# A new written order for the first two chunks of a hash-masked attention and MLP kernel, with two transpose banks and casts out of PSUM

## The chip, the cores and the metric

The kernel runs on one core of one Trainium2 chip. The metric is the device time of an execution in microseconds (us); a kernel's time is the median of its runs. A profile is one execution taken by the hardware profiler. Engines are TensorE (PE, with its weight loads as PEld), VectorE (DVE), ScalarE (ACT), GpSimd (POOL) and SyncE (SP). DMAs are issued from SP, ACT or POOL.

## The reference

Four batches, eight heads, 768 positions, head dimension 64. Queries and keys are hashed by the signs of six projections; a key counts for a query only if all six bits agree. The heads are then joined to rows of 512 and go through a normalised two-layer MLP with a residual.

```python
q_bits = (np.einsum('bhsd,dk->bhsk', q, proj) > 0)          # k_bits likewise
mask = q_bucket[:, :, :, None] == k_bucket[:, :, None, :]
scores = np.where(mask, scale * np.matmul(q, k.transpose(0, 1, 3, 2)), -1e9)
attn = np.exp(scores - np.max(scores, axis=-1, keepdims=True))
attn = attn / (np.sum(attn, axis=-1, keepdims=True) + 1e-09)
x = np.matmul(attn, v)                 # heads joined: (4, 768, 512)
xn = (x - mu) / np.sqrt(var + 1e-06) * g_ln
out = x + np.maximum(xn @ w_ch1, 0.0) @ w_ch2
```

## The kernel before

The work is cut into twelve chunks (batch, third), each of 2 x 128 query positions. A chunk's attention is twelve units: `scores` (four matmuls of 256 columns into one of two `sc` tiles), `exps` on ACT, `values` (eight matmuls into `av`) and, every third unit, `divide` on DVE. The mask is part of the scores: the six bits stand as extra rows under the 64 rows of transposed queries and keys in the operand tile `slots0` or `slots1` (even and odd batches), so that a matmul over 70 rows makes score and agreement together. A chunk's MLP (`norm`, eight `up` products with a relu, eight `down` products) runs between the units of the next chunk. From chunk 2 on `interleave` spreads it there together with the preparation of the next batch, which the strings in `steps` place by letters.

Batch 0 and batch 1 are prepared in different ways.

For batch 0 everything is made on the engines, in `first_two`, and the order of the first two chunks is written out by hand in the string `opening`. Each word is one step, in the order in which the engines get their instructions; every engine then works its own queue in order. For a head h, `T` (`transposes`) makes three key blocks and one query block by four PE transposes into a PSUM tile `tpose` of tag `av1`; `E` (`scaled`) copies that to an SBUF tile `qkT` or `spare` with a factor; `C` (`cast`) copies half of it, 64 x 512, from SBUF into `slots0` as bf16; `H` (`hash_two`) multiplies two heads with the projection; `B` (`compare`) turns the products into bits; `O` (`odd_bits`) copies a 6 x 512 strip of bits. The letter behind a word names the engine: a for ACT, d for DVE, g for POOL. `LT`, `LE`, `LC`, `LH`, `LB`, `LO` do the same for the later query blocks of two heads. `S`, `X`, `V`, `D` are the four parts of a unit. `K` are matmuls on constants that keep PE awake, `J` copies the projection, `vc`, `su`, `sd` prepare the values. `n`, `xt`, `xe`, `nr`, `U`, `R` are the MLP of chunk 0 up to its relus. `V` and `T` share the tag `av1`: the first chunk's `av` is in `av0` alone, the second's alternate.

The word `w` issues loads from POOL's queue: `w0` the first MLP weight (two DMAs), `w1` the queries and keys of batch 1, first half, `w2` the second weight (two DMAs), `w3` the second half's queries and keys and the first half's values. The loads of batch 0 go from SP and two from ACT.

For batch 1 and later the operands are made by DMA. `na` (`narrow`) casts a half's queries and keys to bf16 on POOL (into `nat16`, one buffer, which the last three `qkT` of batch 0 share as `spare`). `op` is `operands`, a DMA transpose into `slots1`, and `shifted`, a DMA that moves its upper rows; both are issued from SP. `bl` (`blocks`) are DVE block transposes of the fp32 data, `hashes` multiplies them with the projection and writes the bits to DRAM (`bits_d`), and `bit_rows` reads them back in four DMAs. In the string of chunk 2 the second half follows: narrowing, transpose (`T11`), values (`W11`), shift (`P11`), hashes (`H11`), bit rows (`J11`). In the string of chunk 3, `n` issues the DMA transpose `xnT` of chunk 2's normalised rows, and the next word `L20` loads batch 2, all from SP's queue in that order:

```python
        2: "n d d H10 d d x N11 J10 d N11 B11 d T11 B11 V10 d B11 W11 d B11 u P11 u H11 u J11 E10 u V11 u u u u",
        3: "n L20 d d d d W20 d E11 d N20 d N20 B20 d T20 B20 u B20 u B20 u P20 u u u u u",
```

Of the kernel before, what the change touches and what calls it, by code (L numbers as in the profile page):

```python
# [9 lines left out]
F32 = mybir.dt.float32  # L10
# [20 lines left out]
def kernel(  # L31
# [11 lines left out]
    nc = tc.nc  # L43
# [16 lines left out]
    consts = ctx.enter_context(tc.tile_pool(name="consts", bufs=1))  # L60


    wake = consts.tile([P, P], BF16)
    nc.vector.memset(wake, 2.0 / P)
    wake2 = consts.tile([P, 2], BF16)
    nc.vector.memset(wake2, 0.0)

    proj1 = consts.tile([P, D], F32)
    nc.vector.memset(proj1, 0.0)
    identf = consts.tile([P, P], F32)  # L70
    make_identity(nc, identf)
    nc.gpsimd.dma_start(out=proj1[0:D, 0:n_bits], in_=proj)
    expb = consts.tile([P, 2], F32)
    nc.gpsimd.memset(expb[:, 0:1], -scale * n_bits * 0.25 / Q_SCALE)
    nc.gpsimd.memset(expb[:, 1:2], -scale * n_bits * LBIT)
# [51 lines left out]
    def load_half(b, half):  # L127

        h0 = half * H // 2
        t = {}  # L130
        for nm in "qk":
            t[nm] = nat.tile([P, H // 2, NC, D], F32, tag=f"{nm}nat", name=f"{nm}nat")

        cuts = [[0, 1, 2, 4] if half == 0 else [0, 2, 4], [0, 4], [0, 2, 4], [0, 2, 4]][b]
        for lo, hi in zip(cuts, cuts[1:]):
            for nm, src in (("q", q), ("k", k)):
                eng = nc.gpsimd if b == 1 else nc.scalar if nm == "k" and hi - lo == 1 else nc.sync
                eng.dma_start(
                    out=t[nm][:, lo:hi],
                    in_=src[b, h0 + lo : h0 + hi].rearrange("h (p c) d -> p h c d", p=P),  # L140
                )
        if b == 0 and half == 0:
            nc.scalar.activation(wake2[:, 0:1], wake2[:, 1:2], AF.Exp)
            t["v"] = load_values(b, half)
        return t
# [16 lines left out]
    class Prep:  # L162


        def __init__(self, b):
            self.b, self.tiles = b, {}
            self.sl, self.va, self.vs = slots[b % 2], vaug[b % 2], vsum[b % 2]
            self.qkT, self.nat16, self.bt = {}, {}, {}

        def load(self, half):  # L170
            self.tiles.setdefault(half, {}).update(load_half(self.b, half))
# [16 lines left out]

            return self.sl.rearrange("p h a (c t) -> p h (a c) t", t=P)

        def transposes(self, key):

            tp = ps_av.tile([P, 4, P], F32, tag="av1", name="tpose")
            late = isinstance(key, tuple)
            for g in range(4):
                if late:
                    h, nm, c = 2 * key[1] + g // 2, "q", 2 + 2 * (g % 2)
                else:
                    h, nm, c = key, "kkkq"[g], 2 * (g % 3)
                nc.tensor.transpose(  # L200
                    tp[:, g, :],
                    self.tiles[h // 4][nm][:, h % 4, c : c + 2].rearrange("p c d -> p (c d)"),
                    identf,
                )
            self.bt[key] = tp

        def scaled(self, key, engine):

# [30 lines left out]

        def cast(self, key, par, engine):  # L240

            self.copy_by(
                engine,
                self.places(key, slice(0, D), par),
                self.as_placed(key, self.qkT[key][par * D : (par + 1) * D]),
            )

        def hash_two(self, keys):

# [25 lines left out]

        def narrow(self, half, a):

            if a == 0:
                self.nat16[half] = work.tile(
                    [P, H // 2, 2, NC, D], BF16, tag="nat16", bufs=1, name="nat16"  # L280
                )
            nc.gpsimd.tensor_copy(self.nat16[half][:, :, a], self.tiles[half]["qk"[a]])  # L282
# [134 lines left out]
    def att_units(b, t, x):  # L417
# [15 lines left out]
        for j in range(NP):  # L433
# [7 lines left out]
            for g, grp in enumerate(groups):  # L441
# [18 lines left out]
                    )  # L460
                    state[g] = ex

                def values(grp=grp, g=g, state=state, j=j, ha=ha):
                    if g == 0:
                        slot = 0 if (b, t) == (0, 0) else j % 2
                        av = ps_av.tile([P, 2, TT, D1], F32, tag=f"av{slot}", name="av")
                        state["av"] = av
                        if b == 0:
                            nc.tensor.matmul(
                                av,  # L470
                                epsk,
                                vsplit[:, ha : ha + 2, :].unsqueeze(2).to_broadcast(
                                    [P, 2, TT, D1]
                                ),
                                start=True, stop=False, skip_group_check=True,
                            )
# [39 lines left out]
    def mlp_steps(b, t, x):  # L516
        st = {}
        steps = []

        def norm_rows(i):  # L520

            if i == 0:
                st["xn"] = work.tile([P, ND, TT, P], BF16, tag="xn", bufs=1, name="xn")
                st["mv"] = work.tile([P, TT, 2], F32, tag="mv", name="mv")
            xn, mv = st["xn"], st["mv"]
            stats = work.tile([P, 6], F32, tag="stats", bufs=4, name="stats")
            nc.vector.bn_stats(stats, x[:, i, :])  # L527
            nc.vector.bn_aggr(mv[:, i, :], stats)  # L528
            nc.vector.scalar_tensor_tensor(  # L529
                xn[:, :, i, :],  # L530
                x[:, i, :].rearrange("p (o d) -> p o d", d=P),
                mv[:, i, 0:1],
                gbc.rearrange("p (o d) -> p o d", d=P),
                op0=AOP.subtract, op1=AOP.mult,
            )
# [6 lines left out]

        def norm():

            for i in range(TT):
                norm_rows(i)
            if b or t > 1:
                xnT = work.tile([P, ND, CT], BF16, tag="xnT", bufs=1, name="xnT")
                nc.sync.dma_start_transpose(
# [12 lines left out]
                        tp[:, dt, i * P : (i + 1) * P], st["xn"][:, dt, i, :], ident  # L562
                    )

        def xcopy():

            st["xnT"] = work.tile([P, ND, CT], BF16, tag="xnT", bufs=1, name="xnT")
            nc.vector.tensor_copy(st["xnT"], st["tp"])

        def up_products(n2):  # L570
            if n2 == 0:
# [41 lines left out]
        def down(i, part):  # L613
# [20 lines left out]
            (870, lambda i=i, part=part: down(i, part)) for i in range(TT) for part in range(4)  # L634
        ]
        parts = {
            "rows": norm_rows, "scale": norm_scale, "xt": xtrans, "xe": xcopy,
            "up": up_products, "relu": rectify, "columns": down_columns,
        }

# [86 lines left out]
    def chunk_tile():  # L727
# [4 lines left out]
    mlp = {0: mlp_steps(*chunks[0], xs[0])}  # L732

    opening = """
        K26 T0 E0a C0.0a C0.1d K6 T1 E1a C1.1a C1.0d K10 J0 H0 K10 T2 B0 E2a B1 O0a K8 T3 C2.0g
        O1d S0 E3a C2.1d vc0 w0 S1 X0 C3.1d H1 C3.0d X1 su0 B2 T4 sd0 S2 O2a E4a B3 S3 V0 X2
        C4.0g O3d T5 C4.1d V1 w1 E5a V2 S4 X3 C5.0d H2 C5.1d vc1 D2 X4 LT2 B4 S5 LE2a su1 B5 O4g
        X5 T6 O5g sd1 S6 V3 LC2.1g E6a LC2.0d S7 X6 C6.1d C6.0g T7 V4 w2 E7d V5 X7 S8 C7.0d H3
        C7.1d X8 D5 LT0 B6 V6 LE0a V7 B7 O6g LT1 O7d LC0.0g S9 LE1d LC0.1g V8 S10 X9 LC1.1d LH0
        w3 D8 X10 LC1.0d S11 LB0 V9 X11 V10 LO0d LT3 LB1 S12 LE3a V11 LO1d S13 X12 LC3.0g D11  # L740
        LH1 n0 LC3.1g X13 S14 V12 X14 V13 n1 S15 X15 V14 S16 LB2 xt0 nr0 X16 D14 V15 xe0 S17
        LO2g V16 LB3 X17 U0 LO3d S18 R0d U1 na0 X18 bl3 S19 U2 R1a bl0 X19 S20 R2d U3 na1 op0
        bl1 V17 S21 R3a D17 V18 X20 U4 bl2 V19 X21 U5 R4d S22 R5a V20 S23 X22 D20 V21 U6 X23 V22
        S24 R6d V23 X24 U7 D23 R7a
    """

    def first_two():
# [6 lines left out]
        nc.sync.dma_start(out=gbc, in_=moe_g_ln.partition_broadcast(P))  # L754
        every = units[0] + units[1] + units[2][:1]
        parts = mlp[0][4]
        engines = {"a": nc.scalar, "d": nc.vector, "g": nc.gpsimd}

        def keep_awake(n):
            tp = ps_mm.tile([P, P], F32, tag="mm", name="wakep")  # L760
# [19 lines left out]
        def both(i):  # L780
# [2 lines left out]
        table = {  # L783
            "K": lambda n: keep_awake(n),
            "J": lambda n: first_head_projection(),
            "T": lambda h: prep.transposes(h),
            "E": lambda h, e: prep.scaled(h, e),
            "C": lambda h, par, e: prep.cast(h, par, e),
            "H": lambda j: prep.hash_two([2 * j, 2 * j + 1]),
            "B": lambda h: prep.compare(h),  # L790
            "O": lambda h, e: prep.odd_bits(h, e),
            "LT": lambda j: prep.transposes(("late", j)),
            "LE": lambda j, e: prep.scaled(("late", j), e),
            "LC": lambda j, par, e: prep.cast(("late", j), par, e),
            "LH": lambda i: prep.hash_two(both(i)),
# [4 lines left out]
            "V": lambda u: every[u][2](),  # L800
# [5 lines left out]
            "n": lambda i: parts["rows"](i),  # L806
            "nr": lambda _: parts["scale"](),
            "xt": lambda _: parts["xt"](),
            "xe": lambda _: parts["xe"](),
# [4 lines left out]
            "op": lambda _: (nxt.operands(0), nxt.shifted(0)),  # L814
        }
        for word in opening.split():
            name = word.rstrip("0123456789.adg") if word[-1] in "adg" else word.rstrip("0123456789.")
            rest = word[len(name) :]
            engine = [engines[rest[-1]]] if rest[-1] in engines else []
            numbers = [int(x) for x in rest.rstrip("adg").split(".")]  # L820
            table[name](*numbers, *engine)


# [275 lines left out]
```

## Time and profile before

| | us |
|---|---|
| median of 3 runs | 314.08 (313.74 to 314.28) |
| the profiled execution | 312.45 |
| its span, first to last instruction | 310.6 |
| PE busy | 299.4 (96%) |
| ACT busy | 217.2 (70%) |
| DVE busy | 184.6 (59%) |
| POOL busy | 84.7 (27%) |
| granted TensorE clock, mean | 1.00 |

The first opening score matmul starts at 10.94, the last hidden product of chunk 0 (`U7`) at 50.51, and chunk 3 begins at about 78. Busy shares are means over the whole span; in the first 45 us PE is the engine that waits, after that it hardly does. In a line of the timeline the columns are start, duration, engine (SPq is SP's queue), line, operation, output and inputs with shapes, count, and in brackets the idle time before it and what ended it. An issuing instruction's duration is that of the issue, not of the transfer.

### The profile page before, as it was taken

To read this page: it belongs to the slowest core of one execution; us is meant where nothing else is said; L and a number is where in the kernel's file an instruction comes from. 1 tells how busy PE (TensorE), PEld (TensorE's weight loads), DVE (VectorE), ACT (ScalarE), POOL (GpSimd) and SP (SyncE) were. 2 spreads that over 40 slices of the span, in tenths; PEclk is the share of its full clock that TensorE was granted. 3 is DMA by queue.
4 is the path that set the end of the run, shared out by engine and by line. 5 is a ranking of instruction groups with operands and counts; after the bars stand their busy time and mean duration, and the time that the engine had idled before them with its cause. 6 is when DMAs were issued, how large, how long until landed. Compare 5 with 4: busy or idle time off the path is not lost.

```text
span 310.6 us, 7810 instructions
## 1 busy us (share of the span) xinstructions
PE 299.4 (96%) x3241; PEld 226.0 (73%) x3268; DVE 184.6 (59%) x404; ACT 217.2 (70%) x272; POOL 84.7 (27%) x110
## 2 busy tenths in 40 slices
PE   7979999999999999999999999999999999999995
PEld 6656787678669678678679668669679678688574
DVE  1799996654665756743793694653643734734522
ACT  5677977775798777688788778778778677666020
POOL 3467530914321118151290470100100100100200
PEclk9999999999999999999999999999999999999999
DMA  7999998487396476695199637030030110200302
GB/s 237 374 208 304 211 339 129 103 124 185 52 313 156 93 245 119 130 273 154 64 262 154 171 76 168 19 76 37 1 102 0 35 71 0 69 36 0 104 0 77
DMA packets 64970, 40.93 MB, mean 132 GB/s; under 512 B 47153, under 2 KB 59953, under 8 KB 64929
## 3 DMA queue, kind: packets, MB, share of 16 engines
q1 hardware_dynamic: 60224, 31.59, 41.1%
q0 software_dynamic: 4128, 8.13, 11.1%
q10 hardware_dynamic: 576, 0.66, 0.6%
q8 instruction: 27, 0.44, 0.6%
q14 instruction: 15, 0.11, 0.1%
HBM read 27.98 MB, written 6.88 MB: 112 GB/s over the span
## 4 chain that ended last, share of the span: by engine, by line
PE 84%; DVE 9%; ACT 3%; issue 2%; DMA 1%; POOL 0%; SPq 0%; ACTq 0%; POOLq 0%
PE hp L577 26%; PE o L618 22%; PE sc L446 18%; PE av L480 10%; PE hash L321 3%; DVE slots L262 2%; PE tpose L200 1%; DVE slots L238 1%; DVE bt L287 1%; PE wakep L762 1%; PE o L600 1%; PE hash L252 1%; DMA xnT<-xn 1%; DVE xn L529 1%; DVE x L508 1%
## 5 line engine op out<-in xcount | busy, mean ns | idle before, releaser
L456 ACT ACTIVATE ex<-sc,expb 128x1024 bf16<-128x1024 f32 x144 | 159.5, 1113 | 56.5 <-PE sc L446 54.0
L577 PE MATMUL hp<-xnT,w_sb 128*128 128x256 bf16 x768 | 98.7, 272 | 1.6 <-DVE hbuf L587 0.9
L618 PE MATMUL o<-w_sb,hbuf 128*128 128x512 bf16 x341 | 89.6, 379 | 1.2
L446 PE MATMUL sc<-slots 70*128 70x256 bf16 x576 | 86.5, 272 | 2.2 <-POOL slots L238 1.5
L577 PEld LDWEIGHTS <-w_sb 128*128 128x128 bf16 x768 | 72.0, 97 | 11.2 <-issue 2.4
L480 PEld LDWEIGHTS <-ex 128*128 128x128 bf16 x1152 | 54.0, 98 | 15.7 <-ACT ex L456 1.6
L446 PEld LDWEIGHTS <-slots 70*128 70x128 bf16 x576 | 51.8, 97 | 17.2 <-issue 3.7
L480 PE MATMUL av<-vaug,ex 128*128 128x65 bf16 x1152 | 58.8, 194 | 0.3 <-ACT ex L456 0.2
L587 DVE TENSOR_SCALAR hbuf<-hp 128x512 bf16<-128x512 f32 x48 | 32.8, 684 | 43.6 <-PE hp L577 42.5
L618 PEld LDWEIGHTS <-hbuf 128*128 128x128 bf16 x368 | 33.6, 97 | 25.5
L540 POOL TENSOR_SCALAR rs<-mv 128x2 f32<-128x2 f32 x12 | 9.1, 759 | 155.2 <-DVE mv L528 155.2
L589 ACT ACTIVATE hbuf<-hp 128x512 bf16<-128x512 f32 x48 | 28.5, 594 | 20.2 <-PE hp L577 20.2
L623 DVE SCALAR_TENSOR_TENSOR x<-o,rs,x 128x512 f32<-128x512 f32 x23 | 17.1, 744 | 26.4 <-PE o L618 23.5
L529 DVE SCALAR_TENSOR_TENSOR xn<-x,mv,gbc 128x512 bf16<-128x512 f32 x24 | 17.9, 751 | 0.8
L508 DVE TENSOR_TENSOR x<-x,rc 128x256 f32<-128x256 f32 x36 | 16.8, 466 | 1.2
L500 DVE TENSOR_SCALAR rc<-av 128x4 f32<-128x4 f32 x36 | 5.7, 158 | 19.8 <-PE av L480 19.8
L527 DVE BATCH_NORM_STATS2 stats<-x 128x6 f32<-128x512 f32 x24 | 16.5, 690 | 0.4
L351 POOL CAST vaug<-vnat 128x1536 bf16<-128x1536 f32 x8 | 12.0, 1494 | 15.6 <-DMA vnat<-in_v_dram 15.6
L501 DVE TENSOR_TENSOR x<-av,vsum 128x256 f32<-128x256 f32 x36 | 14.9, 414 | 0.0
L282 POOL CAST nat<-qnat 128x1536 bf16<-128x1536 f32 x6 | 8.8, 1470 | 16.8 <-issue 8.8
L180 ACT ACTIVATE knat<-knat 128x768 f32<-128x768 f32 x16 | 13.4, 836 | 0.0
L180 ACT ACTIVATE qnat<-qnat 128x768 f32<-128x768 f32 x16 | 13.3, 833 | 0.0
(86 smaller groups left out, 215.9 us busy)
## 6 DMA issues: line engine op xcount, KB each, us to landing
out_dram<-x SPq DMA_DIRECT2D x23, 256.0 KB
vnat<-in_v_dram SPq DMA_DIRECT2D x7, 768.0 KB
qnat<-in_q_dram SPq DMA_DIRECT2D x11, 384.0 KB
knat<-in_k_dram SPq DMA_DIRECT2D x11, 384.0 KB
w_sb<-in_moe_w_ch_dram POOLq DMA_DIRECT2D x4, 1024.0 KB, 14.4
slots<-slots SPq DMA_DIRECT2D x6, 384.0 KB
qnat<-in_q_dram POOLq DMA_DIRECT2D x2, 768.0 KB, 14.8
knat<-in_k_dram POOLq DMA_DIRECT2D x2, 768.0 KB, 16.0
```

The source lines that it names most:

```text
L180: nc.scalar.activation(src, src, AF.Square, accum_out=sq[:, a, col : col + 1],)
L446: nc.tensor.matmul(sc[:, i, :], key_block(h, kj), query_blocks(h),)
L456: nc.scalar.activation(ex, sc, AF.Exp, bias=expb[:, 1:2] if b else expb[:, 0:1], scale=scale if b else scale / Q_SCALE,)
L480: nc.tensor.matmul(av[:, h - ha, qi, :], state[g][:, i, qi * P : (qi + 1) * P], va[:, h, kj, :], start=(b > 0 and (g, i, qi) == (0, 0, 0)) ...
L508: nc.vector.tensor_tensor(xv, num, rc.unsqueeze(3).to_broadcast([P, 2, TT, D]), op=AOP.mult)
L527: nc.vector.bn_stats(stats, x[:, i, :])
L529: nc.vector.scalar_tensor_tensor(xn[:, :, i, :], x[:, i, :].rearrange("p (o d) -> p o d", d=P), mv[:, i, 0:1], gbc.rearrange("p (o d) -> p ...
L577: nc.tensor.matmul(hp[:, i, :], w1_sb[:, dt, nt * P : (nt + 1) * P], st["xnT"][:, dt, :], start=(dt == 0), stop=(dt == ND - 1),)
L587: nc.vector.tensor_scalar_max(dst, src, 0.0)
L589: nc.scalar.activation(dst, src, AF.Relu)
L618: nc.tensor.matmul(o2, st["h"][:, nt, i * P : (i + 1) * P], w2_sb[:, nt, :], start=(nt == 0), stop=(nt == NH - 1),)
L623: nc.vector.scalar_tensor_tensor(x[:, i, :], o2, st["rs"][:, i : i + 1], x[:, i, :], op0=AOP.mult, op1=AOP.add,)
```

## The change

The string `opening` is replaced. With it `transposes` may use either of two PSUM tags (`T1d`, `LT0`: a letter behind `T` or `LT` picks `av0`), and `values` may take the other of its two. A cast that DVE makes now reads the PSUM tile `tpose` and scales on the way, not the SBUF copy; casts of ACT and POOL still read the copy. Eleven of the twelve `O` steps are on POOL, one on ACT; DVE has three casts and seven scalings. Of the 60 keep-awake matmuls 26 stay. The two norm rows take their statistics first and are centred after. The projection is loaded from ACT's queue, not POOL's. In the new string `w1`, `w2` and `w3` stand later, and `na0`, `na1` and `op0` are almost the last words.

```diff
-    nc.gpsimd.dma_start(out=proj1[0:D, 0:n_bits], in_=proj)
...
         if b == 0 and half == 0:
+            nc.scalar.dma_start(out=proj1[0:D, 0:n_bits], in_=proj)
             nc.scalar.activation(wake2[:, 0:1], wake2[:, 1:2], AF.Exp)
...
-        def transposes(self, key):
+        def transposes(self, key, bank=None):
-            tp = ps_av.tile([P, 4, P], F32, tag="av1", name="tpose")
+            tp = ps_av.tile([P, 4, P], F32, tag="av0" if bank else "av1", name="tpose")
...
-            self.bt[key] = tp
+            self.bt[key] = self.tp[key] = tp
...
         def cast(self, key, par, engine):
-            self.copy_by(
-                engine,
-                self.places(key, slice(0, D), par),
-                self.as_placed(key, self.qkT[key][par * D : (par + 1) * D]),
-            )
+            dst, rows = self.places(key, slice(0, D), par), slice(par * D, (par + 1) * D)
+            if engine is nc.vector:
+                nc.vector.tensor_scalar_mul(
+                    dst, self.as_placed(key, self.tp[key][rows]), HALF_SCALE
+                )
+            else:
+                self.copy_by(engine, dst, self.as_placed(key, self.qkT[key][rows]))
...
-                def values(grp=grp, g=g, state=state, j=j, ha=ha):
+                def values(other=False, grp=grp, g=g, state=state, j=j, ha=ha):
                     if g == 0:
-                        slot = 0 if (b, t) == (0, 0) else j % 2
+                        slot = (0 if (b, t) == (0, 0) else j % 2) ^ other
...
-            for i in range(TT):
-                norm_rows(i)
+            for step in (row_stats, row_centred):
+                for i in range(TT):
+                    step(i)
...
     opening = """
-        K26 T0 E0a C0.0a C0.1d K6 T1 E1a C1.1a C1.0d K10 J0 H0 K10 T2 B0 E2a B1 O0a K8 T3 C2.0g
-        O1d S0 E3a C2.1d vc0 w0 S1 X0 C3.1d H1 C3.0d X1 su0 B2 T4 sd0 S2 O2a E4a B3 S3 V0 X2
-        C4.0g O3d T5 C4.1d V1 w1 E5a V2 S4 X3 C5.0d H2 C5.1d vc1 D2 X4 LT2 B4 S5 LE2a su1 B5 O4g
-        X5 T6 O5g sd1 S6 V3 LC2.1g E6a LC2.0d S7 X6 C6.1d C6.0g T7 V4 w2 E7d V5 X7 S8 C7.0d H3
-        C7.1d X8 D5 LT0 B6 V6 LE0a V7 B7 O6g LT1 O7d LC0.0g S9 LE1d LC0.1g V8 S10 X9 LC1.1d LH0
-        w3 D8 X10 LC1.0d S11 LB0 V9 X11 V10 LO0d LT3 LB1 S12 LE3a V11 LO1d S13 X12 LC3.0g D11
-        LH1 n0 LC3.1g X13 S14 V12 X14 V13 n1 S15 X15 V14 S16 LB2 xt0 nr0 X16 D14 V15 xe0 S17
-        LO2g V16 LB3 X17 U0 LO3d S18 R0d U1 na0 X18 bl3 S19 U2 R1a bl0 X19 S20 R2d U3 na1 op0
-        bl1 V17 S21 R3a D17 V18 X20 U4 bl2 V19 X21 U5 R4d S22 R5a V20 S23 X22 D20 V21 U6 X23 V22
-        S24 R6d V23 X24 U7 D23 R7a
+        K26 J0 T0 T1d E0a LT0 E1a C1.1g C0.1g C1.0a H0 C0.0a T2d E2a LE0d B0 B1 T3 O0g S0 LT1d O1g
+        S1 C3.0p C2.0g E3a H1 X0 vc0 S2 T5 C2.1g LE1d X1 B2 T4d C3.1a E5a O2g B3 E4d su0 S3 O3a T6d
+        w0 sd0 X2 H2 C5.0a V0d E6d B4 V1 T7d S4 C4.0g E7d C5.1g C6.1g X3 C4.1g O4g X4 V2 S5 vc1
+        C7.1p C7.0p H3 B5 B7 B6 X5 S6 V3 V4 O5g O6g V5 su1 S7 X6 S8 C6.0g D5 X7 LH0 sd1 V6 LC0.1g S9
+        D2 X8 O7g V7 S10 LB0 X9 LT3 LB1 LC0.0g X10 V8 S11 LE3d LO0g LT2 LC1.1g D8 X11 S12 V9 LE2d
+        V10 X12 V11 S13 S14 LC1.0g D11 V12 n0 LO1g n1 LC2.0g X13 X14 LH1 ns0 S15 ns1 S16 X15 V13 LB2
+        w1 V14 xt0 LC2.1g S17 LO2g V15 LB3 xe0d X16 X17 bl0 LO3g V16 S18 U0 U1 X18 V17 LC3.1g R0a
+        S19 LC3.0g U2 bl1 X19 D14 S20 V18 w2 R1d U3 S21 V19 R2d R3a U4 X20 R4d U5 V20 S22 X21 U6 R5d
+        nr0 X22 R6a w3 S23 bl3 U7 D20 S24 na0 X23 D17 V21 V22 R7d bl2 V23 na1 op0 X24 D23
     """
```

More of the change, by code (lines that the diff above doesn't have):

```diff
@@ L60 @@
     consts = ctx.enter_context(tc.tile_pool(name="consts", bufs=1))
+    proj1 = consts.tile([P, D], F32)
+    nc.vector.memset(proj1, 0.0)
     wake = consts.tile([P, P], BF16)
@@ L66 @@
     nc.vector.memset(wake2, 0.0)
-    proj1 = consts.tile([P, D], F32)
-    nc.vector.memset(proj1, 0.0)
     identf = consts.tile([P, P], F32)
     make_identity(nc, identf)
-    nc.gpsimd.dma_start(out=proj1[0:D, 0:n_bits], in_=proj)
     expb = consts.tile([P, 2], F32)
@@ L167, in __init__ @@
             self.sl, self.va, self.vs = slots[b % 2], vaug[b % 2], vsum[b % 2]
-            self.qkT, self.nat16, self.bt = {}, {}, {}
+            self.qkT, self.nat16, self.bt, self.tp = {}, {}, {}, {}
         def load(self, half):
@@ L276, in narrow @@
         def narrow(self, half, a):
-            if a == 0:
+            if half not in self.nat16:
                 self.nat16[half] = work.tile(
@@ L518, in mlp_steps, with row_stats @@
         steps = []
-        def norm_rows(i):
+        def row_stats(i):
             if i == 0:
@@ L524, in norm_rows @@
                 st["mv"] = work.tile([P, TT, 2], F32, tag="mv", name="mv")
-            xn, mv = st["xn"], st["mv"]
+            mv = st["mv"]
             stats = work.tile([P, 6], F32, tag="stats", bufs=4, name="stats")
@@ L528, in norm_rows, with row_centred @@
             nc.vector.bn_aggr(mv[:, i, :], stats)
+        def row_centred(i):
+            xn, mv = st["xn"], st["mv"]
             nc.vector.scalar_tensor_tensor(
@@ L563, in xtrans, with xcopy @@
                     )
-        def xcopy():
+        def xcopy(engine=nc.vector):
             st["xnT"] = work.tile([P, ND, CT], BF16, tag="xnT", bufs=1, name="xnT")
-            nc.vector.tensor_copy(st["xnT"], st["tp"])
+            if engine is nc.scalar:
+                nc.scalar.activation(st["xnT"], st["tp"], AF.Copy)
+            else:
+                nc.vector.tensor_copy(st["xnT"], st["tp"])
         def up_products(n2):
@@ L636, in mlp_steps @@
         parts = {
-            "rows": norm_rows, "scale": norm_scale, "xt": xtrans, "xe": xcopy,
+            "stats": row_stats, "centred": row_centred, "scale": norm_scale, "xt": xtrans, "xe": xcopy,
             "up": up_products, "relu": rectify, "columns": down_columns,
@@ L756, in first_two @@
         parts = mlp[0][4]
-        engines = {"a": nc.scalar, "d": nc.vector, "g": nc.gpsimd}
+        engines = {"a": nc.scalar, "d": nc.vector, "g": nc.gpsimd, "p": nc.vector}
         def keep_awake(n):
@@ L785, in first_two @@
             "J": lambda n: first_head_projection(),
-            "T": lambda h: prep.transposes(h),
+            "T": lambda h, bank=None: prep.transposes(h, bank),
             "E": lambda h, e: prep.scaled(h, e),
@@ L791, in first_two @@
             "O": lambda h, e: prep.odd_bits(h, e),
-            "LT": lambda j: prep.transposes(("late", j)),
+            "LT": lambda j, bank=None: prep.transposes(("late", j), bank),
             "LE": lambda j, e: prep.scaled(("late", j), e),
@@ L799, in first_two @@
             "X": lambda u: every[u][1](),
-            "V": lambda u: every[u][2](),
+            "V": lambda u, bank=None: every[u][2](bank is not None),
             "D": lambda u: every[u][3](),
@@ L805, in first_two @@
             "w": loads,
-            "n": lambda i: parts["rows"](i),
+            "n": lambda i: parts["stats"](i),
+            "ns": lambda i: parts["centred"](i),
             "nr": lambda _: parts["scale"](),
             "xt": lambda _: parts["xt"](),
-            "xe": lambda _: parts["xe"](),
+            "xe": lambda _, e: parts["xe"](e),
             "U": lambda n2: parts["up"](n2),
@@ L816, in first_two @@
         for word in opening.split():
-            name = word.rstrip("0123456789.adg") if word[-1] in "adg" else word.rstrip("0123456789.")
+            name = word.rstrip("0123456789.adgp") if word[-1] in engines else word.rstrip("0123456789.")
             rest = word[len(name) :]
             engine = [engines[rest[-1]]] if rest[-1] in engines else []
-            numbers = [int(x) for x in rest.rstrip("adg").split(".")]
+            numbers = [int(x) for x in rest.rstrip("adgp").split(".")]
             table[name](*numbers, *engine)
```

## The prediction, made before the changed kernel was run

> **What bounds the kernel now.** Times are us. I read the page first, then the chain of waits, then the timelines of VectorE (DVE), GpSimd (POOL) and SyncE (SP) over the first 92 us. The chain by engine says that TensorE (PE) ends everything:
>
> ```profile
> PE 84%; DVE 9%; ACT 3%; issue 2%; DMA 1%; POOL 0%; SPq 0%; ACTq 0%; POOLq 0%
> ```
>
> Past 45 us PE is busy almost without a break, so the change, which touches the first 50 us, can pay only in PE waits and PE work taken out there, and only if nothing later takes the lead back. In the opening the waits are DVE's, and DVE's are POOL's. The timeline of DVE:
>
> ```profile
> 10.30 0.42 DVE L238 CAST slots<-qkT 64x512 bf16<-64x512 f32 x1
> 11.61 1.97 DVE L238 CAST slots<-qkT 64x512 bf16<-64x512 f32 x2 [0.89 <-ACT qkT L217]
> 17.24 2.87 DVE L238 CAST slots<-spare 64x512 bf16<-64x512 f32 x2 [0.39 <-ACT spare L217]
> ```
>
> The same SBUF-to-SBUF cast takes 0.42 alone, and 1.97 and 2.87 for two while POOL runs its value cast. Over the opening those excesses sum to some 4.7. What pays the lead back stands in the timelines of POOL and SP:
>
> ```profile
> 24.27 1.99 POOL L658 DMA_DIRECT2D w_sb<-in_moe_w_ch_dram  x2
> 29.87 0.77 POOL L138 DMA_DIRECT2D qnat<-in_q_dram  x1
> 38.95 1.47 POOL L282 CAST nat<-qnat 128x1536 bf16<-128x1536 f32 x1
> 40.36 1.53 POOL L282 CAST nat<-knat 128x1536 bf16<-128x1536 f32 x1
> ...
> 41.92 7.75 SPq L304 DMA_TRANSPOSE slots<-nat  x1
> 53.64 0.73 SPq L312 DMA_DIRECT2D slots<-slots  x1
> 57.15 0.38 SPq L334 DMA_DIRECT2D bits_d<-bits  x1
> 60.10 3.14 SPq L340 DMA_DIRECT2D slots<-bits_d  x4
> 63.29 3.75 SPq L304 DMA_TRANSPOSE slots<-nat  x1
> 68.91 0.69 SPq L312 DMA_DIRECT2D slots<-slots  x1
> 76.33 3.04 SPq L340 DMA_DIRECT2D slots<-bits_d  x4
> 82.46 1.29 SPq L549 DMA_TRANSPOSE xnT<-xn  x1
> ```
>
> This is one serial queue that prepares batch 1. Its head, the operand transpose, waits for POOL's two narrowing casts; each later step waits for a landing before it. In the semaphore records the transpose lands at 53.62, the shift at 58.05, the bits (queued behind the shift's packets) at 60.03, the second transpose at 68.85, the second shift at 76.02, the second bits at 76.28. So from the first landing to the end of the last bit-row issue (76.33+3.04=79.37) it takes 25.75, whatever PE does. Only then can SP issue the xnT transpose of chunk 2 and the loads of batch 2. Today SP is not late there: the xnT transpose was ready at 82.40, when DVE ended the norm, so the queue has 3.0 to spare. But what follows has none:
>
> ```profile
> 87.03 0.98 DVE L287 STREAM_TRANSPOSE bt<-qnat 128x768 f32<-128x768 f32 x1 [1.01 <-DMA qnat<-in_q_dram]
> ...
> 91.13 0.98 DVE L287 STREAM_TRANSPOSE bt<-qnat 128x768 f32<-128x768 f32 x1
> ```
>
> DVE waits 1.01 for the first load of batch 2, and the second block transpose starts at 91.13 on a load landed at 91.11, where DVE was free at 91.01. Behind it stands a relu, and PE, with two buffers for the hidden products, waits for that relu. So a later xnT issue at SP is a later end, one for one.
>
> **The change, part by part.** I laid out each engine's written order, every instruction beginning when its engine is free and what it waits for has ended, with the durations of the rows. The old order laid out so puts the last hidden product of the opening at 50.2 (trace 50.51), so I trust such a time to about half a us there.
>
> *PE.* 34 of 60 keep-awake matmuls go; warm ones are 56 ns apart: 1.9. Between the first transposes and the first hidden product the old layout holds 6.7 of PE waits, the new one 4.3. With smaller pieces PE enters chunk 2 some 4.7 early. The rows that carry it: the exponentials (1.11 each) run from about 11.1 instead of 11.64, then sixteen in a row.
>
> *DVE.* Fourteen SBUF casts become three from PSUM, and seven instead of two scalings (0.69) come to it. A 64x512 cast out of PSUM is not in the trace; the nearest rows are 0.42 (from SBUF, alone) and 0.69 (L262, 38x512 out of PSUM; L219 is the same). I take 0.69; at 0.42 three casts would gain 0.8, beside other work. The price of the second bank, values and transposes sharing it, is inside the PE waits above.
>
> *POOL.* It now carries eleven of the twelve odd-bit copies and most casts. Between its w1 load and its w2 load stand 21 of them (0.61 to 0.69, with the gap 0.64: 13.4), the value cast (1.5) and the q and k loads of batch 1 (1.7): 16.6 at least. So w2, issued at 24.27 today, cannot go before some 32.5. In the layout it goes at 36.1: POOL stands 2.4 idle before an odd-bit copy whose compare waits on DVE behind both norm rows. Behind w2 wait the next q, k, v loads (29.87 today, 39.5 then) and the two narrowing casts, which now come last: operand transpose issued at 44.9, not 41.92 (41.1 if POOL never waited).
>
> *The loads' landing.* In the old trace w2 lands 10.05 after the load ahead of it, then q, k and v 6.4 later, at 49.18. From 36.1, with about 2.5 to the first data (bounds 2 and 3.2, the 3.2 being the 192 KB load on ScalarE, ACT, issued 0.73, landed 3.9), v lands at 36.1+2.5+10.05+6.4=55.1.
>
> *The transpose.* Alone it lands 5.56 after issue (63.29 to 68.85). The one issued at 41.92 took 11.70: its first packets ran at 46.1, when POOL's loads ran dry, and it landed 4.44 after the last of them. Bounds for the new one: 44.9+11.7=56.6 if it takes as long as before, 55.1+4.44=59.5 if it again waits for the loads. I take 58.5, two thirds of the way, because that is what its packets did. The Trainium skill (DMA: Bandwidth & Descriptors, Queues, rings and completion order) says that a DMA engine takes turns between queues, a packet of some 9 to 17 descriptors at a time, so a transpose should not have to wait for another queue to run dry. By it the landing would be at the early bound; the trace agrees only in part, with no transpose packet for about 3 us after 43.
>
> *The sum.* 58.5+25.75=84.25 for the xnT issue, against 82.46: 1.8 later, and with it the loads, the block transposes and the end. PE's 4.7 of lead turns into waits between 65 and 95, and 1.8 on top.
>
> *Small parts.* The projection on ACT's queue costs ACT one issue of 0.45; with the table load (1.28) ACT is ready by 3.9, and its first input is there at 4.5: nothing, 0.6 of cover. It lands between 4.9 (the load ahead of it) and 7.0 (issue plus POOL's 5.4); the next transposes wait for a load landed at 8.15 anyway. POOL's 0.75 saved hides likewise. The interleaved norm rows are the same six instructions (3.31 today): nothing, between minus 0.2 and plus 0.2, on DVE.
>
> The profiled execution took 312.45, span 310.6 and 1.85 around it; the median of the runs is 314.08, 1.6 above. The differences hold for both, and I predict the median: 314.08+1.8=315.9.
>
> **Rivals.** *Faster: the queue keeps its slack.* POOL waits less than in my layout; DVE no longer holds it up, as it did when the cast at 10.30 took POOL 0.89. The point that decides is a landing of the first transpose before 56.7 (53.62+3.0). With POOL never idle the transpose is issued at 41.1 and v lands at 32.5+2.5+16.45=51.5, so the transpose lands between 52.8 (11.7 after issue) and 55.9 (4.44 after v); two thirds of the way, as in the forecast, is 54.9, and the xnT issue at 80.65, 1.8 earlier than now: 312.3. Against it: the compare stands behind the norm rows by the written order. If the queue did not matter at all, 309.4, the whole lead. Chance 0.22.
>
> *No change: turns.* The transpose lands at 56.6 among the loads, and lead and delay cancel: 314.0. The rule above speaks for it, the packets against. Chance 0.15.
>
> *Slower still: POOL is the bound.* If its copies take 0.69 to 0.72, as some do today, 21 of them add 1.7 ahead of w2: 317.6. Chance 0.13.
>
> *Cold PE.* Until 4.0 matmuls of 128 columns ran 107 ns apart, then 56. With 34 keep-awakes gone, PE is busy only a third of 4 to 7.5; if it fell back, 2.8 of work before 11 would double, and up to 2 of it would reach POOL: 317.9. Its longest wait there is 1.9, so chance 0.05.
>
> **Numbers.** Forecast 0.45. Slower in all 0.63, same 0.15, faster 0.22; the same is within 0.2% (0.63 us), about what a measurement here can tell. The forecast's own range, from landings of 57.7 to 59.5, is 315.1 to 316.9. For 8 in 10 I take 312.3, where POOL never waits, to 317.8; left out are a lead kept whole and slowdowns stacked.
>
> **What would show it.** Right: w2 issued near 36, the operand transpose near 45 and landed near 58.5, the first xnT transpose (L549's successor) issued straight after the last bit rows at about 84, PE 4 to 5 early at 50 and idle some 6 between 65 and 95. Wrong: the transpose landing before 57, SP idle before that xnT transpose, or PE still early at 100; or PE not early at 50 at all.

## The result, and the profile after

The changed kernel takes 322.91 us (median; 319.81 to 323.93) against 314.18 (313.74 to 314.46): 8.7 slower, a ratio of 1.027 (95% interval 1.0234 to 1.0306). The direction was forecast, the size was not: 315.9 was predicted, in a range up to 317.8. The profiled execution took 323.56, its span 321.8, so 11.2 more than the old span. Of these, 1.7 lie behind the last computing instruction, where the last store lands (4.5 here, 2.8 before the change; 2.8 to 4.5 over all traces); 9.5 are in the work. Where one run of a kernel lay more than 1.5% above the fastest of that kernel, as in three experiments below, its median is that of the other runs.

Where the 9.5 arise is seen by following one instruction through both traces. These are the starts of hidden products (L577, now L587) by their number in the chunk whose MLP they belong to:

| product | before | after | difference |
|---|---|---|---|
| chunk 0, first | 39.35 | 34.73 | -4.6 |
| chunk 0, last | 51.28 | 44.91 | -6.4 |
| chunk 1, first | 65.08 | 64.75 | -0.3 |
| chunk 1, 33rd | 73.35 | 74.35 | +1.0 |
| chunk 2, first | 89.37 | 92.64 | +3.3 |
| chunk 2, 17th | 92.74 | 99.48 | +6.7 |
| chunk 2, 33rd | 95.42 | 103.81 | +8.4 |
| chunk 3, 17th | 116.97 | 126.47 | +9.5 |
| chunk 11, first | 292.81 | 302.34 | +9.5 |

The new opening gains 6.4. All of it and 9.5 more are lost between 45 and 127 us; after that the two kernels run alike. (Of the step to chunk 1, 1.3 is no loss but the new order: with the loads early, below, the same two products differ by that much with no wait between them.) The page's chain by engine now names DMA, which it hardly did before:

```profile
PE 70%; DMA 14%; DVE 6%; SPq 3%; ACT 2%; issue 2%; POOL 2%; ACTq 0%; POOLq 0%; DVEq 0%
```

PE's waits, grouped by what ended them (us in total, times, longest), say which transfers and which engines:

```profile
PE share L367 <- POOL vs L362: 3.5, 2, 1.8
PE o L628 <- DMA w_sb<-in_moe_w_ch_dram: 2.9, 1, 2.9
PE hp L587 <- DVE hbuf L597: 2.8, 2, 2.6
PE hp L587 <- DVE x L633: 2.0, 2, 1.1
```

All four lie past 50 us, and only the second is a load that PE reads itself. The others stand behind POOL and DVE, which wait in their turn. What for is in the timelines of POOL and of SP's queue, the same rows as those shown of before:

```profile
35.61 1.78 POOL L668 DMA_DIRECT2D w_sb<-in_moe_w_ch_dram  x2
38.45 0.84 POOL L137 DMA_DIRECT2D qnat<-in_q_dram  x1
42.19 1.47 POOL L284 CAST nat<-knat 128x1536 bf16<-128x1536 f32 x1
64.56 1.47 POOL L284 CAST nat<-qnat 128x1536 bf16<-128x1536 f32 x1 [13.62 <-DMA slots<-nat]
```

```profile
43.69 17.32 SPq L306 DMA_TRANSPOSE slots<-nat  x1
64.46 0.73 SPq L314 DMA_DIRECT2D slots<-slots  x1
...
72.70 4.37 SPq L306 DMA_TRANSPOSE slots<-nat  x1
...
85.94 3.04 SPq L342 DMA_DIRECT2D slots<-bits_d  x4
89.10 1.29 SPq L556 DMA_TRANSPOSE xnT<-xn  x1
```

The operand transpose is issued at 43.69, 1.8 later than before, but SP goes on to the shift, which waits for its landing, only at 64.46, 10.8 later. From there the serial queue takes 24.52 to the end of its last bit rows at 88.98 (25.75 before), and the xnT transpose of chunk 2 goes at once, at 89.10 (82.46 before). POOL's second narrowing waits 13.62 for the same landing, because it writes the buffer that the transpose reads; the values and value sums queue behind it, and PE waits for those (`share`). The end of the chain is on DVE, which was to wait for the loads of batch 2:

```profile
93.78 0.98 DVE L289 STREAM_TRANSPOSE bt<-qnat 128x768 f32<-128x768 f32 x1 [4.87 <-DMA qnat<-in_q_dram]
...
97.88 0.98 DVE L289 STREAM_TRANSPOSE bt<-qnat 128x768 f32<-128x768 f32 x1 [1.55 <-DMA qnat<-in_q_dram]
```

Both are 6.75 later than before (87.03, 91.13), and so is PE's 17th product of chunk 2.

### The profile page after: what moved, and what is told of

Read it like the earlier page. It is cut to its first block, busy times and chain, and to the rows that moved or that the text cites. A ratio compares the mean times of both kernels' runs of the same rounds, so it can differ in the third digit from the quotient of the medians.

```text
span 321.8 us, 7765 instructions
## 1 busy us (share of the span) xinstructions
PE 301.5 (94%) x3234; PEld 225.6 (70%) x3234; DVE 178.1 (55%) x393; ACT 214.3 (67%) x267; POOL 94.0 (29%) x125
## 4 chain that ended last, share of the span: by engine, by line
PE 70%; DMA 14%; DVE 6%; SPq 3%; ACT 2%; issue 2%; POOL 2%; ACTq 0%; POOLq 0%; DVEq 0%
PE hp L587 22%; PE o L628 17%; PE sc L448 15%; PE av L482 9%; DMA slots<-nat 6%; DMA qnat<-in_q_dram 2%; PE hash L254 2%; PE hash L323 2%; DMA vnat<-in_v_dram 2%; ACT ex L458 2%; DMA proj<-in_proj_dram 2%; DVE bt L289 1%; SPq L306 1%; DMA bits_d<-bits 1%; PE o L610 1%
## 5 line engine op out<-in xcount | busy, mean ns | idle before, releaser
L587 PE MATMUL hp<-xnT,w_sb 128*128 128x256 bf16 x768 | 99.5, 274 | 5.4 <-DVE hbuf L597 2.8
L628 PE MATMUL o<-w_sb,hbuf 128*128 128x512 bf16 x368 | 94.0, 382 | 2.9 <-DMA w_sb<-in_moe_w_ch_dram 2.9
L587 PEld LDWEIGHTS <-w_sb 128*128 128x128 bf16 x768 | 72.7, 98 | 17.6 <-issue 7.7
L597 DVE TENSOR_SCALAR hbuf<-hp 128x512 bf16<-128x512 f32 x49 | 33.6, 686 | 46.8 <-PE hp L587 46.7
L546 POOL TENSOR_SCALAR rs<-mv 128x2 f32<-128x2 f32 x12 | 6.7, 559 | 147.7 <-DVE mv L530 147.5
L510 DVE TENSOR_TENSOR x<-x,rc 128x256 f32<-128x256 f32 x36 | 18.6, 517 | 1.2
L535 DVE SCALAR_TENSOR_TENSOR xn<-x,mv,gbc 128x512 bf16<-128x512 f32 x24 | 16.6, 734 | 0.0
L289 DVE STREAM_TRANSPOSE bt<-qnat 128x768 f32<-128x768 f32 x12 | 11.2, 956 | 6.4 <-DMA qnat<-in_q_dram 6.4
```

What stands on the lines that cost most here:

```text
L510: nc.vector.tensor_tensor(xv, num, rc.unsqueeze(3).to_broadcast([P, 2, TT, D]), op=AOP.mult)
L535: nc.vector.scalar_tensor_tensor(xn[:, :, i, :], x[:, i, :].rearrange("p (o d) -> p o d", d=P), mv[:, i, 0:1], gbc.rearrange("p (o d) -> p ...
L587: nc.tensor.matmul(hp[:, i, :], w1_sb[:, dt, nt * P : (nt + 1) * P], st["xnT"][:, dt, :], start=(dt == 0), stop=(dt == ND - 1),)
L597: nc.vector.tensor_scalar_max(dst, src, 0.0)
L628: nc.tensor.matmul(o2, st["h"][:, nt, i * P : (i + 1) * P], w2_sb[:, nt, :], start=(nt == 0), stop=(nt == NH - 1),)
```

## Experiments

Theory A, formed from these rows: the late loads and the late operand transpose cost everything, and the new opening as such is a gain. Theory B: the new order on the engines costs by itself. Each experiment edits the changed kernel unless it says otherwise; times are medians, with the ratio to the kernel before measured beside them.

**The loads early.**

```diff
-  ... S6 V3 V4 O5g O6g V5 ...  LB2 w1 V14 xt0 LC2.1g S17 LO2g ...  V18 w2 R1d ...  R6a w3 S23 ...
+  ... S6 V3 V4 w1 O5g O6g V5 ...  LB2 w2 V14 xt0 LC2.1g S17 w3 LO2g ...  V18 R1d ...  R6a S23 ...
```

> The changed kernel with the words w1, w2, w3 moved forward in its string: w1 ahead of O5g, w2 where w1 stood, w3 ahead of LO2g; nothing else. Theory A (late loads and the late operand transpose cost everything, the new opening itself is worth its 6.4 us at U7): w1 is issued near 21, w2 near 29, w3 near 33; w2 lands near 43, so the wait of 2.9 at the first down products goes; the operand transpose is issued near 40 and lands near 53; the xnT transpose of chunk 2 goes at about 80, and as SP's chain still sets it, the end is some 3 us ahead of the kernel before: 311 (309.5 to 312.5). Theory B (the new order on the engines itself costs, by its own waits and a slower clock): the loads land as early, but the time stays above 318.

311.24 against 313.44, ratio 0.9906 (0.9869 to 0.9943). SP's queue:

```profile
40.16 12.97 SPq L306 DMA_TRANSPOSE slots<-nat  x1
55.10 0.73 SPq L314 DMA_DIRECT2D slots<-slots  x1
...
79.10 1.89 SPq L556 DMA_TRANSPOSE xnT<-xn  x1
```

This is theory A in each step: no wait for w2, the transpose landed at 55.1 (near 53 expected), the xnT transpose at 79.10, the time within 0.3 of the 311 expected. Three words moved in a string turn 2.7% slower into 0.9% faster.

**The kernel before, with its loads late.**

```diff
-  ... V0 X2 C4.0g O3d T5 C4.1d V1 w1 E5a ...  V4 w2 E7d ...  LE1d LC0.1g ...  LH0 w3 D8 ...  LC3.1g X13 ...  LO2g V16 ...
+  ... V0 X2 C4.0g O3d T5 C4.1d V1 E5a ...  V4 E7d ...  LE1d w1 LC0.1g ...  LH0 D8 ...  LC3.1g w2 X13 ...  LO2g w3 V16 ...
```

> The kernel before with its words w1, w2, w3 moved back, so that the loads are issued at about the changed kernel's times (29, 35.5, 38.5) and the operand transpose near 44; its opening otherwise untouched. Theory A: SP's chain ends as late as in the changed kernel (xnT transpose of chunk 2 near 89, against 82.5), the block transposes of batch 2 come as late, and the time is 321 to 324, with none of the new opening in it. Theory B: the loads are worth the 1.8 us of my forecast at most, 314 to 316.

320.79, ratio 1.0237 (1.0177 to 1.0298): just under the 321 to 324 of theory A, far above the 314 to 316 of theory B. Its opening is the old one (last product of chunk 0 at 50.78), PE never waits for w2, and the end is nearly as late as the changed kernel's:

```profile
43.63 16.95 SPq L304 DMA_TRANSPOSE slots<-nat  x1
63.87 0.73 SPq L312 DMA_DIRECT2D slots<-slots  x1
...
88.40 1.29 SPq L549 DMA_TRANSPOSE xnT<-xn  x1
```

So with the loads late the opening's 6.4 are worth nothing: SP's chain sets when the products of chunk 2 run, whenever PE gets there. It also shows that PE's wait for w2 in the changed kernel was paid almost wholly out of the lead: by the first product of chunk 2 the two kernels are 0.7 apart (91.96 and 92.64), as are their xnT transposes (88.40 and 89.10).

**The second half's loads written behind the transpose**, in the changed kernel (shown) and in the one with early loads, where `w3` is taken from ahead of `LO2g`.

```diff
-  ... nr0 X22 R6a w3 S23 ... na1 op0 X24 D23
+  ... nr0 X22 R6a S23 ... na1 op0 w3 X24 D23
```

> The changed kernel with w3 alone moved, to behind op0: the narrowing casts and the operand transpose go ahead of the loads of queries, keys and values. Theory A1 (the transpose lands 4 us after the loads ahead of it, because its packets get through only when POOL's queue is dry): the transpose is issued near 41.5, its packets run when w2 ends near 50, it lands near 54 and w2 lands some 2 us earlier; the time is 313 to 317. Theory A2 (the transpose is slow by itself in this place): it lands near 62 and the time stays at 320 to 323.

> The first kernel of this group with w3 moved on to behind op0. Theory A: the operand transpose is issued near 38 to 40, lands near 48, SP's chain ends near 74, ahead of the norm that it waited for, and the whole lead of the opening reaches the end: 307 to 309. Rival: the second half's queries, keys and first values now land after 50 and are missed in chunk 2, where POOL narrows and casts them: 311 to 314.

323.12 (1.0301; 1.026 to 1.0343) and 320.72 (1.0186; 1.0126 to 1.0245). Both expectations by my theory failed, and in the second kernel the rival's 311 to 314 too: the transpose lands at 62.90 (64.46 in the changed kernel) and at 63.26 (55.10 with the loads early). Written behind is not issued behind. The transpose waits for the end of POOL's second cast, and POOL issues the loads at that same moment: the first load at 41.56 and 40.02, the transpose at 41.63 and 40.09. So the two run side by side, and these runs do not tell what a transpose issued well ahead of loads would do; the next experiment does. What happens side by side, the DMA view of the changed kernel shows, over 53 to 57 us (packets, MB, share of the 16 engines; q0 is POOL's queue, q1 SP's):

```profile
q0 software_dynamic: 347, 1.40, 94.6%
q1 hardware_dynamic: 348, 0.09, 10.8%
```

One packet of the transpose goes for one packet of the loads. A load's packet here has up to 4608 bytes, a packet of the transpose 256. The kernel before over 42 to 46 us had the loads alone, and over 35 to 37 us the next experiment has the transpose alone:

```profile
q0 software_dynamic: 379, 1.53, 103.1%
```

```profile
q1 hardware_dynamic: 2233, 0.57, 126.4%
```

Alone the transpose moves 1,117 packets per us, beside these loads 87. It has 3,104 packets, so beside loads it does not end before they do, and until then they move 347 packets in 4 us where they moved 379 alone.

**The transpose with no load beside it.** `w1` ahead of `w0`, the narrowing and the transpose early, `w2` and `w3` as late as in the changed kernel.

```diff
-  ... T6d w0 sd0 ...  V4 O5g O6g ...  S14 LC1.0g D11 ...  LB2 w1 V14 ...  LC3.0g U2 ...  V18 w2 R1d ...  nr0 X22 R6a w3 S23 ...  na0 ... na1 op0 ...
+  ... T6d w1 sd0 ...  V4 w0 O5g O6g ...  S14 LC1.0g na0 na1 op0 D11 ...  LB2 V14 ...  LC3.0g w2 U2 ...  V18 R1d ...  nr0 w3 X22 R6a S23 ...
```

> The changed kernel with w1 in the place of w0, w0 ahead of O5g, na0 na1 op0 behind LC1.0g, w2 behind LC3.0g and w3 behind nr0: the operand transpose is issued when no load is queued behind it, and the last two groups of loads as late as in the changed kernel (w2 near 35.5, w3 near 38). Theory A (a transpose is slow because its packets take turns with those of loads, so it ends only when they do): issued near 30, it lands near 38, SP's chain is no longer late, and the lead of the opening reaches the end: 307 to 309, with w2 as late as in the changed kernel. Theory B (what costs is late loads as such: w2 at the first down products, w3 at the narrowing): 312 or more, with a wait for w2 near 50.

313.66, ratio 0.999 (0.9961 to 1.002): neither theory's time. SP's queue:

```profile
31.62 4.83 SPq L306 DMA_TRANSPOSE slots<-nat  x1
38.70 0.73 SPq L314 DMA_DIRECT2D slots<-slots  x1
53.82 0.38 SPq L336 DMA_DIRECT2D bits_d<-bits  x1
...
60.19 3.14 SPq L342 DMA_DIRECT2D slots<-bits_d  x4
...
76.55 3.04 SPq L342 DMA_DIRECT2D slots<-bits_d  x4
80.89 1.29 SPq L556 DMA_TRANSPOSE xnT<-xn  x1
```

Issued 6.3 ahead of w2, with only the last of w0's packets beside its first, the transpose takes 7.1, as theory A says. The values land at 61.49, as late as in the changed kernel (61.25), and yet the time is some 9 lower: late loads as such are not what costs, the late transpose is. But the chain does not move up with the transpose. The next link is the bits, whose hash products PE makes in chunk 2, so they go to DRAM only at 53.82 (57.15 in the kernel before); and beside the loads they take 6.3 to land, at 60.17, against 60.03 before, so the bit rows go no earlier (60.19, before 60.10). Meanwhile the shift took turns with w2 (1,066 packets to 1,065 between 45 and 52 us), PE waited 1.7 for w2, and a lead of 4.4 at the last product of chunk 0 was 1.3 in chunk 1 and 0.6 in chunk 3. In this profile the opening itself gave 2.0 less than the changed kernel's 6.4: PE started slowly, and its first four hash products took 1.98, against 1.08 there.

**The loads of batch 2 ahead of the last bit rows**, with the loads early.

```diff
-        2: "n d d H10 ... P11 u H11 u J11 E10 u V11 u u u u",
-        3: "n L20 d d d d W20 ...
+        2: "n d d H10 ... P11 u H11 u L20 J11 E10 u V11 u u u u",
+        3: "n d d d d W20 ...
```

> The changed kernel with its loads early (as in e1_loads_early), and in the strings of the later chunks the loads of batch 2 (L20) moved from behind the xnT transpose of chunk 2 to ahead of the last bit rows of batch 1 (J11). Theory A (what takes 3 us of the lead between 89 and 95 us in e1_loads_early is that these loads wait behind SP's serial chain): the loads go near 73, the block transposes of batch 2 no longer wait for them, only the xnT transpose stays at about 79, and the lead of 4.7 reaches the end nearly whole: 308.5 to 310. Rival: the loads run beside the second shift and bit rows and push them back by what they save: 311 or more.

310.69, ratio 0.9886 (0.9842 to 0.9929). The block transposes no longer wait, but the bit rows' issue takes 4.98 beside the loads (3.04 before), so the xnT transpose goes at 82.85. The time lies between the two expectations; the rival's mechanism is there, and no difference from 311.24 is shown.

**The small parts alone, in the kernel before.**

```diff
-    nc.gpsimd.dma_start(out=proj1[0:D, 0:n_bits], in_=proj)
...
         if b == 0 and half == 0:
+            nc.scalar.dma_start(out=proj1[0:D, 0:n_bits], in_=proj)
...
-            for i in range(TT):
-                norm_rows(i)
+            for step in (row_stats, row_centred):
+                for i in range(TT):
+                    step(i)
```

> The kernel before with two small parts of the change alone: the projection loaded from ACT's queue, and the norm rows of chunks 1 to 11 with both statistics first. Both theories and my forecast: no difference, 0 within 0.6 us. If the interleaving shortens DVE's way to the xnT transpose of the last chunk it can show as up to 0.2 there.

314.77 against 314.13, ratio 1.003 (1.0006 to 1.0054): 0.6 slower, at the edge of the 0.6 allowed and just clear of the noise. DVE's copy of the projection, before and here:

```profile
7.15 0.17 DVE L776 COPY proj<-proj 64x6 f32<-64x6 f32 x1
```

```profile
8.44 0.17 DVE L781 COPY proj<-proj 64x6 f32<-64x6 f32 x1 [0.86 <-DMA proj<-in_proj_dram]
```

It is 1.3 later, and the last product of chunk 0 is 1.0 later. From chunk 3 to chunk 11 the difference stays at 0.8: the interleaved norm rows neither cost nor gain.

**The projection back on POOL's queue**, on top of the version with the loads of batch 2 ahead.

```diff
     make_identity(nc, identf)
+    nc.gpsimd.dma_start(out=proj1[0:D, 0:n_bits], in_=proj)
...
-            nc.scalar.dma_start(out=proj1[0:D, 0:n_bits], in_=proj)
```

> e5_l20_first (the changed kernel, loads early, loads of batch 2 ahead of the last bit rows) with the projection's load put back on POOL's queue, behind the identity. If the load on ACT's queue is what lands late and at varying times (6.3 to 8.4 in the runs so far), the copy of the projection ends by about 7.2, ACT's table is ready 0.5 earlier, and the time is 310 to 311, 0.3 to 1 below e5_l20_first. If the projection does not matter, the same as e5_l20_first within 0.6.

310.75 against 313.87, ratio 0.9883 (0.9854 to 0.9912): it beats both kernels. Against 310.69 for the version with the projection on ACT's queue no step is shown. In its profile 6.4 of lead at the last product of chunk 0 have become 1.9 by chunk 3, in waits for value sums (2.0) and xnT (0.7) and before a score matmul (1.1).

**Three edits of that version**: VectorE's casts from SBUF again (with `E3a` written ahead of `C3.0p`); the norm of chunk 2 ahead of the last bit rows; the 34 keep-awake matmuls put back.

```diff
-            if engine is nc.vector:
-                nc.vector.tensor_scalar_mul(
-                    dst, self.as_placed(key, self.tp[key][rows]), HALF_SCALE
-                )
-            else:
-                self.copy_by(engine, dst, self.as_placed(key, self.qkT[key][rows]))
+            self.copy_by(engine, dst, self.as_placed(key, self.qkT[key][rows]))
```

> e8_best with VectorE's three casts reading the SBUF copy again (and E3a written ahead of C3.0p, since the copy must exist). My forecast took 0.69 for a cast out of PSUM against 0.42 from SBUF alone: U7 comes at the same time within 0.8. Rival: PSUM casts are what makes the opening short; U7 then comes 2 or more later.

```diff
-        2: "... H11 u L20 J11 E10 u V11 u u u u",
-        3: "n d d d d W20 ...
+        2: "... H11 u L20 E10 u V11 u u u u",
+        3: "n J11 d d d d W20 ...
```

> e8_best with the last bit rows of batch 1 (J11) moved behind the norm of chunk 2, so that SP issues the xnT transpose ahead of them. If SP's order is all that still takes the lead back, the xnT transpose goes near 78 to 79, PE no longer waits for it, and the time is 308.5 to 310. Rival: the bit rows, now landing near 85, are missed by chunk 3's scores of heads 4 to 7: no gain over e8_best.

```diff
-  ... LT0 E1a C1.1g C0.1g C1.0a H0 C0.0a T2d E2a ...
+  ... LT0 K6 E1a C1.1g C0.1g C1.0a K10 H0 K10 C0.0a T2d K8 E2a ...
```

> e8_best with the 34 keep-awake matmuls put back between the first steps (6, 10, 10, 8). Forecast: at 56 ns each they cost up to 1.9 us at U7, less where PE would wait there anyway. Rival: they keep the clock up (in several runs the matmuls between 4 and 7 us ran at half speed) and cost nothing or gain up to 1.

The casts: 311.42 (0.9899; 0.9863 to 0.9936), the last product of chunk 0 1.3 later in the one profile of each: more than the 0.8 I allowed, less than the rival's 2. The norm first: 312.32 (0.9932; 0.9897 to 0.9967). xnT goes at 78.32, and the rival holds: chunk 3's scores stand 2.9, until 86.64, after the bit rows whose issue ended at 85.22. The keep-awakes: 311.37 (0.9917; 0.9887 to 0.9947), the same product 0.9 later, half of the 1.9 forecast. No step of the time is shown for the first and the last, and their products say little: with the norm first, whose opening is unchanged, the same product is 0.7 later as well.

## Why the prediction was right in its direction and wrong in its size

**Right.** *PE's lead*: 4.7 forecast on entering chunk 2, 4.6 found at the first hidden product of chunk 0 and 6.4 at its last. *The cast out of PSUM*: 0.69 taken, 0.68 to 0.69 found. *POOL*: w2 at 36.1 forecast, 35.61 found; the idle time before an odd-bit copy 2.4, found 2.27; the next loads 39.5, found 38.45; the operand transpose 44.9, found 43.69. *The chain*: 25.75 from the first landing to the end of the last bit rows, found 24.52 (64.46 to 88.98). The nearness is in part luck: "whatever PE does" was misread, since SP had waited 2.7 of the 25.75 for the bits that DVE makes from PE's hash products (until 57.13), and now they go straight behind the shift, at 65.29. *One for one*: the xnT transpose went 6.64 later, the block transposes 6.75. The point that decides, a landing before 56.7, also fits: 55.10 with the loads early is a gain, 62.90 and later a loss; no run in this order lies between.

**The step that failed: the loads' landing, and the transpose's with it.** I took w2's 10.05 and the 6.4 of queries, keys and values from the old trace and added them, with 2.5 to the first data, to the new issue: w2 at 48.7, v at 55.1, then 58.5 for the transpose. In the new trace w2 lands at 54.56, when PE's wait for it ends, and v at 61.25. So the 6.4 held (6.69), and w2's term was the mis-sized one: 18.95 from issue to landing, where I had 12.55. The transpose lands 3.2 after v, at 64.46: the upper bound's rule (4.44 after the last load) was about right, its base was short by 6.2. Two things made w2 slow, and neither is in the old rows. First, w2 was queued behind other loads there and ran at full rate from the start; here POOL's queue had run dry, and its packets of 37 to 39 us were 138, against 390 over 31 to 33 before. Second, from 48 us on the loads shared the engines with the transpose, packet by packet. As an estimate, the first is worth some 2.3 (1,692 packets took from 37 to 48, and at 195 per us they need 8.7), which leaves some 4 to the second.

**The rule I had weighed.** The Trainium skill (DMA: Bandwidth & Descriptors, Queues, rings and completion order) says that an engine takes turns between queues. The trace agrees, 347 packets to 348. What I made of it was wrong: I read turns as an early landing, and gave that case 0.15. Turns by packets of 256 and 4608 bytes mean 3,104 turns at 87 per us, 36 us, so the transpose waits for the loads after all, and they for it. The old trace had not spoken against turns either. I took the first packets at 46.1 as a sign that the loads had run dry; but they came 4.3 after the issue, and in the new trace they come 4.3 after it too, at 48.0, with w2 still running.

**What the sum left out.** (1) w2 has a reader of its own. The down products of chunk 0 waited 2.93 for it, and I never asked who reads w2. In the end it cost little, since the lead paid, as the old opening with late loads shows. (2) The clock. PE's pauses were followed by half speed; mean granted clock is the third number from the right:

```profile
51.60:54.60 3.00, 0.08 (x1) 0.00 (x0) 0.21 (x1) 1.11 (x1) 0.00 (x0) 1.00 1.06 344
54.60:56.00 1.40, 1.40 (x11) 0.76 (x11) 0.00 (x0) 0.00 (x0) 0.00 (x0) 0.74 1.00 362
56.00:57.20 1.20, 1.20 (x8) 0.51 (x6) 0.61 (x2) 0.00 (x0) 0.00 (x0) 0.50 1.05 380
```

The second such pause, before the 17th product of chunk 2, costs 1.6 from there to the 33rd. My cold-PE rival had the mechanism, but only for the first 11 us. Half speed there shows in two other profiles of the new opening, with the transpose alone and with the loads of batch 2 ahead: the first four hash products took 1.98 and 1.95, against 1.08 here, and the last product of chunk 0 came at 46.89 and 46.96, against 44.91. (3) DVE held PE another 1.1 in chunk 3. One of its multiplications took 1.53 there, and 0.42 in the kernel before. POOL's narrowing cast ran beside it now, and before only from 115.27, after it:

```profile
113.51 0.42 DVE L508 TENSOR_TENSOR x<-x,rc 128x256 f32<-128x256 f32 x1
```

```profile
121.69 1.47 POOL L284 CAST nat<-qnat 128x1536 bf16<-128x1536 f32 x1 [7.47 <-issue]
121.91 1.53 DVE L510 TENSOR_TENSOR x<-x,rc 128x256 f32<-128x256 f32 x1
```

That the cast stretches it is argued from the overlap, which other runs bear out: in the old opening with late loads the multiplication took 1.04 beside the cast and the step was 0.6; with the second half's loads written behind, the cast came after it, it took 0.42, and there was no step.

With (2) and (3) the sum closes: 1.8 forecast, 6.0 from the landing, less 1.2 for the shorter chain, 0.1 between xnT and the products, 1.6 for the clock and 1.1 for DVE make 9.4 of the 9.5.

**The small part.** I gave the projection's move 0.6 of cover and a landing of 7.0 at most. In the old opening its copy ran at 8.44 and the median rose by 0.6, with the norm rows changed too: there the cover was too thin. With the new opening the copy ran at 6.3 to 7.2 from either queue, and no price is shown.

**Open.** In the last 3 us of the loads (58 to 61) the packets of the transpose took 40 to 180 ns each in the mean, against 18 once it ran alone; no run tells why. Undoing the second PSUM bank was not tried: the new string needs it.

## What to carry to other kernels

A transfer that is written later is not only later: it meets other traffic, and a duration read where it ran alone or on a full queue no longer holds. Before adding a lead gained early to the end, follow the serial queue that prepares the next stage: here three words in a string decided between 2.7% slower and 0.9% faster, with the same opening. For each moved load ask who reads it first, what shares its engines, and what pauses it makes, since PE ran at half clock behind pauses of 1.8 us and more here.

## What the runs showed of the hardware

A DMA transpose of 256-byte packets beside loads of 4608-byte packets gets one packet for one: 87 per us, against 1,117 alone. A POOL queue that had run dry needed some 5 us to come to its rate: 39, 99, 169, 169, 184 and 200 packets in the six us from 37, against 390 in two us on a full queue. PE's clock fell to 0.50 in or behind nine pauses of 1.76 to 4.87 us in these runs, for 3.4 us in seven places and 6.8 in two, and stayed at 1.00 at pauses of 1.65, 1.72 and 1.75; but no sharp limit follows, for in one opening it fell behind a pause of 1.53. The Trainium skill (TensorE: Matmul & The Clock Gate, Part 1: The HAM clock gate) gives an idle window of about 3.4 us; the runs here show shorter pauses to be enough.
